# A SwiGLU kernel on one core: the steady order of its instructions searched anew, three sums moved from GpSimd to VectorE, and other work in the lead-in

## The chip, the core and the metric

The kernel runs on one core of one Trainium2 chip. The metric is the device time of one execution in microseconds (us), lower is better. The core has a matrix engine (TensorE, in the profile PE, with its weight loads shown apart as PEld), VectorE (DVE), ScalarE (ACT), GpSimd (POOL) and SyncE (SP), which here only issues DMAs. Each engine works through its own instructions in the order in which they were written, and waits at an instruction until what it needs is there.

## The reference, cut to what matters

```python
# x (8, 4096, 192): a causal convolution of 7 taps, the weights a softmax per head (8 heads of 24)
w = exp(weight - max); w = w / (w.sum(-1) + 1e-9)
y[b, s, h, g] = sum_k w[h, k] * x_pad[b, s + k, h, g]
# 32768 tokens of 192: RMS norm, then a gated feed-forward layer
xn = y / sqrt(mean(y * y) + 1e-6) * rms_g
g, val = xn @ w_gate, xn @ w_val          # 192 -> 1536 each
out = (g * sigmoid(g) * val) @ w_out      # 1536 -> 192
```

All inputs and the output are float32; the three weight matrices arrive as float64 words that the kernel converts itself.

## The kernel before

**Tiling.** The 32768 tokens are 32 pairs (0 to 31) of two 512-token tiles. The 1536 hidden units are 12 blocks of 128, taken as 6 double blocks, numbered j = 0 to 5. Pair 0 goes through plain matrix products: the gate loop `plain` (L1099) and the output loop `outer`. Pair 1 has plain gate products (L890, words a to d of the list PLAIN) and the output steps described below. Pairs 2 to 31 are the steady part: for each j the 2x2 block product (two token tiles by two hidden blocks) is done in the Strassen-Winograd manner.

**Gate products.** A *product* (`product`, L918; words P1..P7, Q1..Q4 and A, B, E with a cell letter) is 6 matmuls: three parts of a split operand, two halves of the rows (gate and value). The token operand is split into three parts by `split` (acts n, l, d: a cast on ACT at L683, a subtraction at L826, a multiply-subtract on DVE at L828) after the four sums x1..x4 of the token tiles (`x_sum`, L840). The weights come in pieces of 192 KB from a DRAM scratch `wd` through `ring`, ten slots in SBUF. `ring_load` (L798) fills a slot; SP issues it right behind the last product of the piece that held the slot, so each piece is asked for when the tenth-last one is done with. The first ten are issued at the word R (`ring_start`). The memory of the ring is lent before that: pair 2's tokens lie in it (`tokens`).

**Sums of the products.** Products of one j add up in PSUM in four cells a, b, c, d, each cell in one of four double banks (`open` takes one, `give` returns it). f1 (ACT, L683) copies cell a to b, f3 copies c to SBUF (two of the nine columns of `tt`, called s5), f4 (DVE, L989) makes c = b + s5, f5 makes d = b + s5. For each cell, g (ACT, L995) takes the silu of the gate half, m (DVE, L1002) multiplies it with the value half into `ht` and so frees the bank.

**Output.** The acts h1 to h4 (L972, DVE or POOL) sum cells of `ht` for the Strassen output; a *step* `o<form>.<k>` (`step`, `tiles`, `tile`, L945; form 1 to 7, k the double block) is 12 matmuls of 32 columns of weights. The forms accumulate in X, Y and Z; forms 1 and 7 with k = 0 start a bank afresh. C22 and C21 (DVE, L1019), the copies c1, s7, c2 (ACT) and the transposes T11 to T22 (DVE, L960) put the result together in `o_sb`; `st` (`leave`, L1051) stores it.

**The next pairs, meanwhile.** ld (`load_part`, L154) loads x of a pair two ahead, cv.0 to cv.6 (L453) are the taps for the next one, sq, red, pow, bc, mul the norm, pl (`put_away`, L1062) writes normed tokens to a DRAM scratch, ft (`fetch`, L654) reads them back as `xb`. ft.1 and ft.3 do nothing, since ft.0 and ft.2 fetch both halves.

**What sets the order.** From pair 1 on the order is written by hand. LINE is the order of a pair's work on PE. The lists FIRST (pass 1) and ORDER (each pass from 2 on) hold words that are carried out one after the other: `p3` emits the next three items of the pair's PE line; a word such as `Vf4.0` has the engine's letter (V DVE, G POOL, A ACT, S a DMA that SP issues), the act and its index; `+` and `++` mean the next pair or the one after it, `-` the one before; W is the next piece of the weights' preparation in the lead-in (`prepare`, which splits the weights and writes `wd`). A pass ends in the middle of its pair's output: pass w starts on PE with two products of pair w (P5.0, P1.0) and the six o3 steps of pair w-1, then come 66 products and 36 steps.

**Lead-in.** `first_loads` does not exist yet: `load_in` and `load_out` issue the first weight loads ahead of `conv_first`, which convolves pair 0 on ACT with PE's sums (taps 0, 2, 4) and on DVE (taps 1, 3, 5, 6, of which `give` = 2 heads are taken over from ACT's last). `hold` (L226) is a small copy that ties the first weight load to the x rows, since the load needs its result's place. START and LATER are two orders of the lead-in's parts; a letter O in LATER is one step of a converted w_out block (the result, `wo_sb`, is written at L337).

Of the kernel before, what the change touches and what calls it, by code (L numbers as in the profile page):

```python
# [20 lines left out]
def kernel(  # L21
# [10 lines left out]
    nc = tc.nc  # L32
# [3 lines left out]
    H, K = weight.shape  # L36
# [21 lines left out]
    PAIRS = B * NB  # L58
# [18 lines left out]
        "a5 b5 c5 d5",  # L77
    )
    ORDER = (
# [30 lines left out]
    )  # L110
    LINE = (
# [50 lines left out]
    def load_part(p, h, eng):  # L162

        if h == 0:
            x_sb[p] = xs.tile([P, TB + HALO, GS], F32, name="xh")
        load_head(p, p // NB, (p % NB) * PT, h, eng)
# [57 lines left out]
    def hold(t):  # L224

        nc.scalar.copy(out=t, in_=x0[:, -t.shape[1] :, 0])  # L226
# [163 lines left out]
    def conv_first(mine, share, give):  # L390
# [5 lines left out]
        for i, k in enumerate([theirs[0], mine[-1]] + theirs[1:]):  # L396
# [4 lines left out]
            if k == theirs[-1]:  # L401
                cuts = (0, H // 2, H - give)
# [11 lines left out]
        for k in mine:  # L414
            xk = t[:, k : k + NJ, :]
# [428 lines left out]
    class Pair:  # L844
        def __init__(self, p):
            self.p = p
            self.bk, self.o_sb, self.sg = {}, {}, {}
            self.open_half, self.turned = {}, [0, 0]
            self.line = self.products()
# [76 lines left out]
        def step(self, form, k):  # L926
# [3 lines left out]
            fresh = form in (1, 7) and k == 0  # L930
# [127 lines left out]
    def put_away(p, h, eng):  # L1058
        if h == 0:
            scr[p] = dram.tile([D, PT], F32, name="xd")  # L1060
# [101 lines left out]
    def done(it):  # L1162
# [14 lines left out]
        (30, "s"), (35, "v"), (45, "v"), (47, "O"), (50, "O"), (53, "O"), (55, "n"), (60, "t"),  # L1177
# [13 lines left out]
    load_in(0, nc.sync)  # L1191
    load_out(0)
    load_out(1)
    load_in(1, nc.sync)
# [111 lines left out]
```

## Time and profile before

| | |
|---|---|
| median of 3 runs | 2470.25 us (2469.66 to 2471.25) |
| profiled execution | 2473.39 us, its span 2471.6 |
| granted PE clock | 1.000 |
| PE matmuls | L918 12240 records, 1422.0 us busy; L945 16200 records, 1068.8 us |
| DVE | taps 336.6 us (186), silu products L1002 498.0 (744), f4/f5 295.8 (240) |
| POOL | sums L972 427.2 us (300), splits l.0 (L826) 69.7 (29), token norm L503 89.9 (30) |
| DMA | queue q1 425.21 MB, 66.5% of the 16 engines' span; 1440 ring loads, 240 put-aways, 192 loads of x |

How to read it: the span is from the first to the last instruction of the profiled execution, and that execution's time stands beside it. Busy shares are over the whole span. A matmul's record ends where a model puts it, so PE shows as busy through short waits; a weight load (PEld) shows the wait ahead of it. Each group in a view has its start, its busy time, the engine, what it writes and the line; in brackets is idle time ahead of it and what ended that. L683 and L972 are lines that several acts share, so they are told apart by their tiles.

### The profile page before, as it was taken

How to read it: one execution, taken by the hardware profiler on the slowest of the kernel's cores; microseconds unless marked ns; L12 is line 12 of the kernel's file. 1: busy time of each engine (PE TensorE's matmuls, PEld its weight loads, DVE VectorE, ACT ScalarE, POOL GpSimd, SP SyncE). 2: the span in 40 equal slices, each digit the busy share in tenths (PEclk: the TensorE clock that was granted, in tenths of full speed). 3: DMA queues.
4: the chain of work that ended last, by engine and by line, in shares of the span. 5: the costliest groups of instructions: out<-in, count | busy, mean ns of one | idle time of the engine just before them, and what ended most of it. 6: DMA issues, size and time to landing. Idle time of an engine off the chain costs nothing.

```text
span 2471.6 us, 69198 instructions
## 1 busy us (share of the span) xinstructions
PE 2452.5 (99%) x29136; PEld 1894.3 (77%) x29136; DVE 2024.1 (82%) x2530; ACT 1016.2 (41%) x1431; POOL 833.3 (34%) x624
## 2 busy tenths in 40 slices
PE   8999999999999999999999999999999999999999
PEld 5547778887777777877777778777787787777777
DVE  8688888889888789888888787888888888888864
ACT  6443434433344434344334344333444343443332
POOL 0541343423343323334333434233433333333322
PEclk9999999999999999999999999999999999999999
DMA  7364678666677666786667776666776666876653
GB/s 152 60 207 125 175 184 211 179 171 170 164 200 195 181 165 172 176 207 181 190 158 178 179 202 186 176 168 168 199 197 187 165 172 169 203 192 188 159 161 95
DMA packets 716392, 430.55 MB, mean 174 GB/s; under 512 B 510330, under 2 KB 702386, under 8 KB 716082
## 3 DMA queue, kind: packets, MB, share of 16 engines
q1 hardware_dynamic: 712336, 425.21, 66.5%
q8 instruction: 230, 3.77, 0.7%
q10 hardware_dynamic: 3746, 0.92, 0.2%
q14 instruction: 80, 0.66, 0.1%
HBM read 366.96 MB, written 58.98 MB: 172 GB/s over the span
## 4 chain that ended last, share of the span: by engine, by line
PE 90%; DVE 3%; DMA 3%; SPq 1%; issue 1%; POOL 1%; ACT 1%; DVEq 0%; POOLq 0%; ACTq 0%
PE ps L918 55%; PE ps L945 35%; DMA xb<-xd 1%; DMA ht<-in_moe_w_val_dram 1%; DMA ring<-wd 1%; SPq L154 0%; DVE ht L972 0%; POOL part L775 0%; SPq L238 0%; DVE ht L1117 0%; DVE ht L1002 0%; DVE part L771 0%; DVE y L453 0%; DMA x<-in_x_dram 0%; DVE ps L989 0%
## 5 line engine op out<-in xcount | busy, mean ns | idle before, releaser
L918 PE MATMUL ps<-part,ring 64*128 64x512 f32 x12240 | 1422.0, 389 | 2.6 <-DMA ring<-wd 1.9
L918 PEld LDWEIGHTS ps<-part,ring 64*128 64x128 f32 x12240 | 1152.9, 184 | 257.8 <-DVE ps L989 12.5
L995 ACT ACTIVATE tt<-ps 128x512 f32<-128x512 f32 x744 | 438.9, 599 | 715.8 <-PE ps L918 661.7
L1002 DVE TENSOR_TENSOR ht<-ps,tt 128x512 f32<-128x512 f32 x744 | 498.0, 686 | 254.3 <-ACT tt L995 252.2
L945 PE MATMUL ps<-ht,wo_sb 128*32 128x384 f32 (+2 forms) x7272 | 468.3, 380 | 0.8 <-POOL wo_sb L337 0.8
L972 POOL TENSOR_TENSOR ht<-ht 128x512 f32<-128x512 f32 x180 | 272.2, 1520 | 543.9 <-PE ps L945 536.4
L945 PE MATMUL ps<-ht,x 128*32 128x256 f32 (+2 forms) x6696 | 439.1, 379 | 1.3 <-DVE ht L972 1.3
L945 PEld LDWEIGHTS ps<-ht,wo_sb 128*32 128x32 f32 x7272 | 325.1, 110 | 114.5 <-issue 14.5
L945 PEld LDWEIGHTS ps<-ht,x 128*32 128x32 f32 x6696 | 299.6, 110 | 90.9 <-DVE ht L972 1.6
L989 DVE TENSOR_TENSOR ps<-ps,tt 128x1024 f32<-128x1024 f32 x240 | 295.8, 1233 | 54.3 <-ACT tt L683 22.8
L453 DVE SCALAR_TENSOR_TENSOR y<-xh,tp,y 128x1536 f32<-128x1536 f32 x186 | 336.6, 1810 | 0.2
L683 ACT COPY ps<-ps 128x1024 f32<-128x1024 f32 (+1 forms) x151 | 134.6, 891 | 408.0 <-PE ps L918 336.5
L972 POOL TENSOR_TENSOR hs<-ht 128x512 f32<-128x512 f32 x120 | 155.0, 1292 | 262.6 <-DVE ht L1002 262.6
L683 ACT COPY tt<-ps 128x384 f32<-128x384 f32 (+1 forms) x182 | 151.7, 833 | 218.6 <-PE ps L945 154.9
L482 POOL TENSOR_SCALAR r<-r 128x8 f32<-128x8 f32 x31 | 6.1, 197 | 504.5 <-DVE r L477 504.4
L945 PE MATMUL ps<-hs,x 128*32 128x128 f32 (+2 forms) x2232 | 161.4, 379 | 0.0
L972 DVE TENSOR_TENSOR ht<-ht 128x512 f32<-128x512 f32 x192 | 135.0, 717 | 15.2 <-PE ps L945 12.6
L945 PEld LDWEIGHTS ps<-hs,x 128*32 128x32 f32 x2232 | 106.9, 110 | 29.6
L828 DVE SCALAR_TENSOR_TENSOR part<-part,xb 128x1024 fp32r<-128x1024 f32 x87 | 120.1, 1381 | 0.0
L972 DVE TENSOR_TENSOR ht<-hs,ht 128x512 f32<-128x512 f32 x156 | 109.2, 747 | 11.3 <-PE ps L945 10.7
L826 POOL TENSOR_TENSOR part<-xb,part 128x1024 fp32r<-128x1024 f32 x29 | 69.7, 2403 | 124.0 <-PE ps L918 82.1
L503 POOL TENSOR_TENSOR xh<-y,s 128x1536 f32<-128x1536 f32 x30 | 89.9, 2995 | 15.1 <-DVE s L495 8.6
(133 smaller groups left out, 1417.6 us busy)
## 6 DMA issues: line engine op xcount, KB each, us to landing
ring<-wd SPq DMA_DIRECT2D x1440, 192.0 KB
xb<-xd SPq DMA_DIRECT2D x60, 512.0 KB
xd<-xh SPq DMA_DIRECT2D x240, 96.0 KB
xh<-in_x_dram SPq DMA_DIRECT2D x192, 105.0 KB
xb<-xd SPq DMA_DIRECT2D x60, 256.0 KB
out_dram<-o_sb SPq DMA_DIRECT2D x126, 96.0 KB
out_dram<-o_sb SPq DMA_DIRECT2D x62, 128.0 KB
wd<-part SPq DMA_DIRECT2D x5, 1152.0 KB
```

Source lines behind the costliest of these rows:

```text
L453: nc.vector.scalar_tensor_tensor(out=y, in0=xk, scalar=w, in1=y, op0=ALU.mult, op1=ALU.add)
L482: nc.gpsimd.tensor_scalar(out=r, in0=r, scalar1=s / D, scalar2=s * 1e-6, op0=ALU.mult, op1=ALU.add)
L503: e.tensor_tensor(out=yn[p].rearrange("p a t -> p t a"), in0=y, in1=ss[:].rearrange("p (t o) -> p t o", o=1).to_broadcast([P, TB, GS]), op ...
L683: nc.scalar.copy(out=dst, in_=src)
L826: e.tensor_tensor(out=split_of(g, 1).bitcast(F32R), in0=src, in1=high, op=ALU.subtract)
L828: nc.vector.scalar_tensor_tensor(out=split_of(g, 2).bitcast(F32R), in0=high, scalar=1.0 + SPLIT, in1=src, op0=ALU.mult, op1=ALU.subtract,)
L918: nc.tensor.matmul(out=self.both(j, c)[:, h, :], lhsT=left[HALF[h]], rhs=right[HALF[h]], start=(first and q == 0), stop=True, skip_group_c ...
L945: nc.tensor.matmul(out=self.acc(b)[i * Q : (i + 1) * Q, at : at + n], lhsT=left, rhs=cols, start=fresh, stop=True, skip_group_check=True, ...
L972: engine[eng].tensor_tensor(out=dst, in0=a, in1=b, op=op)
L989: nc.vector.tensor_tensor(out=self.both(j, c), in0=self.both(j, "b"), in1=s5, op=ALU.add)
L995: nc.scalar.activation(out=tt[:, t, :], in_=self.both(j, c)[:, 0, :], func=AF.Silu)
L1002: nc.vector.tensor_tensor(out=self.hv(j, "abcd".index(c)), in0=self.both(j, c)[:, 1, :], in1=tt[:, t, :], op=ALU.mult,)
```

## The change

ORDER and LINE are replaced by another order of the same work, and a list SECOND of its own is put in for pass 2. In the new LINE the steps o1.2 and o1.1 stand between the gate products Q2.5 and P4.5; before, all 36 steps followed all products. The steps may now come in any order within a form (`step` marks a bank as begun at its first use). x3, x4 and l.0 are on DVE instead of POOL in the steady passes, and all h4 sums on DVE; of the h sums DVE has 13 and POOL 11 as before, but others. All seven taps for pair w+1 now fall in pass w; before, the first three were done in pass w-1. Stores come one by one, An.0 (the cast of the tokens' first part) is moved behind Ac1, the empty ft.1 and ft.3 are dropped. In FIRST the taps of pair 3 and Vd.2+ (a split of pair 2) go out, Vma.1 and Vmb.1 stand ahead of some W; Vd.2 of pair 2 now comes in SECOND. PLAIN takes up the old order of the output steps, for pair 1. In the lead-in, `hold` copies on VectorE instead of ScalarE, the first weight loads are issued after DVE's first tap, one head (instead of two) of ACT's last tap goes to DVE, and three steps O come earlier.

The lists are cut here; of SECOND, which is nearly the same as ORDER, only the beginning stands.

```diff
     PLAIN = (
         "a0 b0 c0 d0 o1.0 a1 b1 c1 d1 o1.1 a2 b2 c2 d2 o1.2 a3 b3 c3 d3 o1.3 a4 b4 c4 d4 o1.4",
-        "a5 b5 c5 d5",
+        "a5 b5 c5 d5 o7.0 o7.4 o1.5 o7.3 o7.1 o7.2 o2.5 o2.0 o7.5 o6.1 o6.5 o6.0 o6.4 o6.2",
...
     ORDER = (
-        "p2 Vl.2 VC22- VT11- p3- Vd.4 VT22- VT21- Vcv3+ p3- Af1.0 Af3.0 VT12- p4 Aga.0 Vcv4+",
...
-        "Vma.4 Vf5.4 Agb.3 p3 Agd.4 Agc.4 Vmb.3 Vmd.4 Vmc.4 p2 Sft.2+ Sft.3+ Sst0.3- Sld.0++",
-        "Sft.4+ Sft.5+ Agb.4 Sld.1++ Sld.2++ Sst1.1- Gh1.2 Vmb.4 Gh1.1 Gh3.1 Gh1.0 p1 Sld.3++",
-        "Sst0.0- Gh3.2 Sld.4++ Sst0.1- Sld.5++ Af1.5 Sld.6++ Gh1.3 Sld.7++ p1 Af3.5 p2",
-        "Sst1.0- Sst1.2- Sst1.3- Vh1.4 Vh3.4 Vh3.0 Vf4.5 An.0+ Aga.3 p3 Vma.3 p2 Gl.0+ Gh3.3",
-        "Gx3+ Vf5.5 Aga.5 Agc.5 Vma.5 Vmc.5 p3 Vx1+ Agd.5 Agb.5 An.1+ Vx2+ p11 Vmd.5 Vh2.4",
-        "Vmb.5 Vd.0+ Vh1.5 Vh3.5 Vh2.3 Vh2.1 Vh2.5 Gx4+ Gh2.0 An.4+ Ac1 p5 Vh2.2 p1 An.3+ p4",
-        "An.2+ As7 p1 Ac2 Acv0++ Vh4.0 Vd.3+ Vd.2+ p11 Vh4.5 Vl.3+ Vh4.3 Vl.4+ Vcv1++ Vl.1+",
-        "Vcv2++ Vd.1+ p3 Gh4.1 VC21 Gh4.4 Gh4.2",
+        "VC22- p1 p1- VT21- p5- Acv0+ Af1.0 Vd.2 p1 VT22- Af3.0 Vl.2 p2 Vcv1+ VT12- Vf4.0",
...
+        "p1 Agb.4 Vmc.4 Vmb.4 p1 Agd.4 Spl.7+ p2 Af1.5 Sft.2+ Sft.0+ Vmd.4 p4 Af3.5 p1 Vf4.5",
+        "Gh1.3 Aga.5 Sst0.1- p1 Vh3.1 p2 Aga.3 Vma.5 p2 Gh1.4 Vma.3 Vf5.5 p4 Agd.5 Sld.6++ p2",
+        "Vmd.5 Agb.5 Gh3.4 p1 Vmb.5 p1 Vh1.5 Vx3+ Vh3.5 Gh3.3 Vh2.4 Agc.5 p1 Vx1+ Ac1 p1 Vx2+",
+        "p4 Sld.5++ Vx4+ Vh2.0 An.0+ p1 An.3+ Sst0.2- Gh2.1 Vh2.3 Sst1.3- An.4+ Gh2.2 Vd.0+",
...
+        "Vl.0+ Vh4.0 p1 Sft.5+ p2 Vl.4+ Vl.1+ p1 Vl.3+ VT11 Ac2 p2 Vh4.4 p2 VC21 p2 Vd.1+ p1",
+        "p1+ Vh4.5 An.2+",
+    )
+    SECOND = (
+        "p1 VC22- VT11- p3- VT22- Acv0+ VT21- Af1.0 Vd.2 p1- p1 p2- Af3.0 Vl.2 p1 VT12- p1",
...
     FIRST = (
...
-        "Vmc.0 W p1 Gpow+ W W W p1 W p1 Agd.0 W p1 Vmd.0 Vbc+ Vh1.0 p1 Gmul+ p1 Vh3.0 W",
-        "p1 Aga.1 W W W Vma.1 Vh2.0 p1 W W p1 Spl.0+ p1 Agb.1 Vmb.1 Spl.1+ p1 Spl.2+ W p1 Spl.3+ W",
+        "Vmc.0 W p1 Gpow+ W W W p1 W p1 Agd.0 W p1 Vmd.0 Vbc+ Vh1.0 p1 Gmul+ p1 Vh3.0 p1",
+        "Aga.1 Vma.1 p3 Agb.1 Vmb.1 W W W W Vh2.0 W W Spl.0+ Spl.1+ p1 Spl.2+ W p1 Spl.3+ W W",
...
-        "Vx2+ Vh1.4 p2 Gx4+ Vh3.4 Vh2.4 p1 Aga.5 Vma.5 An.3+ p1 An.2+ p1 Vd.3+ p1 Agb.5 Vd.2+",
-        "Vmb.5 Sld.0++ p1 Vl.3+ p2 Vl.1+ Agc.5 Vmc.5 Vd.1+ p1 Sld.1++ Vl.2+ p1 Sld.2++ Agd.5",
-        "p1 Vmd.5 p1 Vh1.5 p2 Ac1 Sld.3++ Vh3.5 Vh2.5 An.0+ An.4+ Gl.0+ Vd.0+ Vl.4+ p3 Sld.4++",
-        "Sld.5++ Sld.6++ Sld.7++ p1 Vh4.5 p1 Vh4.0 R Acv0++ p1 As7 p4 p2 Ac2 p1 Vcv1++ Vcv2++ Vh4.3",
-        "p9 Vh4.2 p2 Vh4.1 p2 VC21 p1 Vh4.4",
+        "Vh3.4 Vh2.4 p1 Aga.5 Vma.5 An.3+ p1 An.2+ p1 Vd.3+ p1 Agb.5 Vmb.5 Sld.0++ p1 Vl.3+",
+        "p2 Vl.1+ Agc.5 Vmc.5 Vd.1+ p1 Sld.1++ Vl.2+ p1 Sld.2++ Agd.5 p1 Vmd.5 p1 Vh1.5 p2",
+        "Ac1 Sld.3++ Vh3.5 Vh2.5 Sld.4++ Sld.5++ Sld.6++ Sld.7++ An.0+ An.4+ Gl.0+ Vd.0+",
+        "Vl.4+ p4 Vh4.5 p1 Vh4.0 R p1 As7 p6 Ac2 p1 Vh4.3 p9 Vh4.2 p2 Vh4.1 p2 VC21 p1 Vh4.4",
+        "Vd.4+ p1+",
     )
     LINE = (
-        "P5.0 P1.0 P2.0 Q1.0 P6.0 Ab.1 Bb.1 Eb.1 P7.0 Q2.0 Aa.1 P3.0 Ea.1 Ba.1 P4.0 Q3.0 Q4.0",
-        "P1.2 Ac.3 P5.2 Bc.3 Ec.3 P6.2 P2.2 Q1.2 Ad.3 Bd.3 P7.2 Q2.2 P3.2 Ed.3 Q3.2 Q4.2 P4.2",
-        "Ac.1 Bc.1 Ec.1 Ad.1 Bd.1 P1.4 Ed.1 P5.4 P6.4 Q1.4 Ab.3 P2.4 Bb.3 P7.4 Q2.4 P3.4 Eb.3",
-        "Q4.4 Q3.4 P4.4 P1.5 Aa.3 Ba.3 P5.5 P6.5 Ea.3 P2.5 Q1.5 P7.5 Q2.5 P3.5 Q3.5 Q4.5 P4.5",
-        "o1.0 o7.0 o1.4 o1.2 o1.3 o1.1 o7.4 o1.5 o7.3 o7.1 o7.2 o2.5 o2.0 o7.5 o6.1 o6.5 o6.0",
-        "o6.4 o6.2 o6.3 o2.3 o4.0 o4.3 o5.2 o5.3 o5.1 o4.5 o5.0 o4.4 o2.2 o4.1 o2.1 o5.4 o4.2",
-        "o5.5 o2.4 o3.3 o3.1 o3.0 o3.5 o3.2 o3.4",
+        "P5.0 P1.0 P6.0 Q1.0 P2.0 Ab.1 P7.0 P3.0 Q2.0 Bb.1 Eb.1 Q4.0 P4.0 Q3.0 Ac.3 Ec.3 Bc.3",
+        "Aa.1 P1.2 Ba.1 Ea.1 P5.2 P6.2 Q1.2 P2.2 Ac.1 Ec.1 Bc.1 P7.2 P3.2 Ad.3 Ed.3 Bd.3 Q2.2",
+        "Q3.2 Q4.2 P4.2 P1.4 Ad.1 Ed.1 Bd.1 P5.4 P6.4 Q1.4 P2.4 Ab.3 Eb.3 P7.4 Bb.3 Q2.4 P3.4",
+        "P4.4 Q3.4 Q4.4 P1.5 Aa.3 Ea.3 P5.5 P6.5 P2.5 Q1.5 Ba.3 P7.5 P3.5 Q2.5 o1.2 o1.1 P4.5",
+        "Q3.5 Q4.5 o1.5 o1.0 o1.3 o1.4 o7.1 o7.2 o2.2 o7.3 o2.0 o2.3 o7.0 o7.4 o2.1 o6.3 o7.5",
+        "o2.4 o6.2 o6.1 o4.1 o4.2 o4.4 o4.3 o6.5 o6.4 o6.0 o2.5 o4.5 o5.2 o5.1 o5.0 o4.0 o5.4",
+        "o5.5 o5.3 o3.0 o3.3 o3.1 o3.2 o3.5 o3.4",
     )
@@ load_part, put_away
-        if h == 0:
+        if p not in x_sb:
             x_sb[p] = xs.tile([P, TB + HALO, GS], F32, name="xh")
...
-        if h == 0:
+        if p not in scr:
             scr[p] = dram.tile([D, PT], F32, name="xd")
@@ hold
-        nc.scalar.copy(out=t, in_=x0[:, -t.shape[1] :, 0])
+        nc.vector.tensor_copy(out=t, in_=x0[:, -t.shape[1] :, 0])
@@ conv_first
-    def conv_first(mine, share, give):
+    def conv_first(mine, share, give, then):
...
-                cuts = (0, H // 2, H - give)
+                cuts = (0, H // 2, H - give) if give else (0, H // 2, H // 2 + 2, H)
...
         for k in mine:
+            if k == mine[1]:
+                then()
@@ class Pair, step
-            fresh = form in (1, 7) and k == 0
+            fresh = (b not in self.begun) and form in (1, 7)
+            self.begun.add(b)
@@ lead-in
-        (30, "s"), (35, "v"), (45, "v"), (47, "O"), (50, "O"), (53, "O"), (55, "n"), (60, "t"),
+        (30, "s"), (33, "O"), (35, "v"), (37, "O"), (44, "O"), (45, "v"), (55, "n"), (60, "t"),
...
-    load_in(0, nc.sync)
-    load_out(0)
-    load_out(1)
-    load_in(1, nc.sync)
-    conv_first((1, 3, 5, 6), 0, 2)
+
+    def first_loads():
+        load_in(0, nc.sync)
+        load_out(0)
+        load_out(1)
+        load_in(1, nc.sync)
+
+    conv_first((1, 3, 5, 6), 0, 1, first_loads)
@@ passes
     run([w for row in FIRST for w in row.split()], 1)
-    for w in range(2, PAIRS + 1):
+    run([w for row in SECOND for w in row.split()], 2)
+    for w in range(3, PAIRS + 1):
         run([w for row in ORDER for w in row.split()], w)
```

More of the change, by code (lines that the diff above doesn't have):

```diff
@@ L848, in __init__ @@
             self.open_half, self.turned = {}, [0, 0]
+            self.begun = set()
+            self.at = {}
             self.line = self.products()
```

39 rows, old and new, of tables (FIRST, ORDER, PLAIN, SECOND) are left out of this document.

## The prediction, on record before the changed kernel ran

> **What bounds the kernel now.** First the page's busy shares and its chain: TensorE (PE) is busy for all but 19 us of the span, and nine tenths of the chain that ended last are its own matmuls. Then the chain in order of time, for one late pass and the end of the lead-in. Then the weight loads in order of time, because a matmul's end is modelled and hides short waits, while a weight load that had to wait shows its idle time. Last, who held SP's queue and PE around the lead-in's end.
>
> ```profile
> PE 2452.5 (99%) x29136; PEld 1894.3 (77%) x29136; DVE 2024.1 (82%) x2530; ACT 1016.2 (41%) x1431; POOL 833.3 (34%) x624
> PE 90%; DVE 3%; DMA 3%; SPq 1%; issue 1%; POOL 1%; ACT 1%; DVEq 0%; POOLq 0%; ACTq 0%
> ```
> ```profile
> 196.01 2.89 DVE ht L972
> ...
> 198.95 15.16 PE ps L945 x184
> 214.10 1.60 PE ps L918 x12
> 215.71 4.04 PE ps L945 x48
> ...
> 2387.10 1.59 PE ps L918 x12
> 2388.68 4.04 PE ps L945 x48
> 2392.72 45.44 PE ps L918 x395
> 2438.16 23.54 PE ps L945 x288
> ```
> ```profile
> 1202.69 1.92 PEld L918 LDWEIGHTS ps<-part,ring 64*128 64x128 f32 x18 [0.28 <-DVE ps L989]
> 1205.01 16.85 PEld L918 LDWEIGHTS ps<-part,ring 64*128 64x128 f32 x150 [0.40 <-DVE ht L1002]
> 1222.01 15.52 PEld L918 LDWEIGHTS ps<-part,ring 64*128 64x128 f32 x138 [0.15 <-ACT ps L683]
> 1237.93 1.91 PEld L918 LDWEIGHTS ps<-part,ring 64*128 64x128 f32 x18 [0.39 <-DVE ps L989]
> ```
> ```profile
> SPq L798 <- DVE part L828: 14.7, 1, 14.7
> ...
> PE ps L918 <- DMA ring<-wd: 1.9, 5, 0.8
> PE ps L945 <- DVE ht L972: 1.3, 1, 1.3
> ```
>
> A pass is four stretches on PE: 2 gate products, 6 output steps, 66 gate products, 36 output steps (12, 72, 396 and 432 matmuls; a few records are missing). Undisturbed, the 150 loads from 1205.01 to 1222.01 are 75 matmul pairs in 17.0 us: 0.227 a pair, 0.68 a product. The two output stretches differ by 30 steps and 19.5 us: 0.65 a step. So the 66 products need 44.95 us, and the thirty long blocks of this trace take 45.44 to 46.83, 45.76 on average. What exceeds is 0.81 a pass, 24.4 us in all. Of it 0.2 a pass is the block's own entry and exit (seen also in the short block, which nothing delays: 1.59 for 6 pairs, 1.36 bare). About 0.03 is jitter. **The remaining 0.58 a pass, 17.4 us in all, is waits, and this is the most that any order can win here.** The loads name them: f4/f5 (L989), a silu product (L1002) that frees a PSUM bank, an ACT copy. The dearest in the bad passes starts as An.0, which holds ACT for the xb fetch in mid-block; f5.5 then comes late.
>
> **Part by part, steady passes.** (1) Switches. The new LINE puts o1.2 and o1.1 between Q2.5 and P4.5, so PE changes from products to steps and back once more in each pass: 31 more switches there and back, counted over both programs (60 product blocks of this kind become 91). One costs 0.22 (short block, 1.59 less 1.36) plus 0.14 (4.04 less 6 times 0.65): 0.36. Together **+11.1 us**. Nothing hides it; PE is the bound.
>
> (2) Waits that go. In the old order Q3.5 follows P7.5 by two products (1.4 us), while f5.5 (1.23) must come between, behind DVE's m.3. The new one has P3.5, Q2.5, o1.2 and o1.1 between P7.5 and P4.5: P7.5's result is there 0.2 us after its end, then DVE has Vh3.1 behind it, m.5 and m.3 (0.60 each), f5.5 (1.23): done 2.0 us after P7.5, and P4.5 starts 3.0 after it. An.0 moves behind Ac1 into the output steps, so the fetch (6.16 us from issue in the chain) has over 6 us before its first reader Vx3, and it is issued behind the gate block's last ring load instead of ahead of five. I laid DVE's other gate work in its new order, each item by its row, (f 1.14 from start to start, m 0.60, tap 1.73, split 1.14, h 0.60), against PE's: f4.0 ends 0.6 before P7.0 needs it, f5.0 0.5 before Q4.0, banks for P1.2, P5.2, P1.4, P5.4, P1.5 and P5.5 come free 0.5 to 1.7 early. The tightest is f3.5 then f4.5 before P7.5, 0.3, the distance it has now without a wait. From m.5 to C22 DVE has 21.1 us of work for 21.9 until o3.0 writes X: 0.7 left. All margins being positive but small, I take 15.5 of the 17.4: **-15.5 us**; ends -8 (half of the waits come back) and -17.4.
>
> (3) The sums that move. DVE gets x3, x4 and l.0 (0.69, 0.69, 1.22), POOL loses them (1.28, 1.30, 2.40). Meetings go: DVE's h ran 1.12 beside POOL's against 0.68, its split 1.71 against 1.22. DVE's load stays near 61 of 74.7 us. Cover: the idle fifth of DVE; without it the 2.6 us would show, as far as it exceeds the 0.7 left before o3.0. **0.**
>
> (4) SP's queue. Loads of the ring (48 a pass) are issued when the tenth-last piece is done with. In the old order each has 6.1 us or more before its use; in the new one six have 4.1 (pieces used from P2.2 through Ac.1, Ec.1 and Bc.1 to P7.2) and four 4.8 to 5.5. Stores go from clusters to single places, and one (0.4 to 1.4 us of issue) stands behind these six. A load alone lands 2.35 us after issue (those at 1284 and 1285, by their semaphores), one queued behind others within half a us 4.2. The six come 0.68 apart: margin 1.5. **0**, bounds 0 to +7.5 (first rival). Put_away moves 8 us later with Gmul, its issues (0.55 each, eight) now beside loads of 5.5 lead; about 0.7 remains.
>
> **The boundary of pass 1 and 2.** Pair 2's tokens lie in the memory that becomes the ring. FIRST no longer has Vd.2+; SECOND has Vd.2, which reads those tokens, so the first ring load waits for it; before, it waited for a split that ended at 200.9. P5.0 of pair 2 stands on PE before the last o3 steps and needs slot 0. From the end E of the steps (214.1 before), DVE has by its rows Vh4.4 from E+0.1 (0.61), Vd.4 (1.14), C22 (0.47), T11, T22, T21 (0.56 each) and Vd.2 (1.22): done at E+5.2. The same first load at 200.9 landed after 2.8, the second, for P1.0, 4.7 after the first issue. So P1.0 starts at E+10.0 instead of E+0.7: **+9.2 us**, ends +7.6 (both land as a lone load) and +9.6. Queued behind it are SP's other loads, which PE gates anyway, and on PE everything.
>
> By the fit in the Trainium skill's SBUF — State Buffer, "The DMA setup-cost knee" (2 us plus bytes at 436 GB/s), a load of 196608 bytes takes an estimated 2.45; the stall would be 7.7 and the sum 1.5 lower. The rows at 200.9 speak against it for loads in a burst, those at 1284 for it.
>
> **Lead-in.** (5) hold on DVE: ACT's taps now start with the first x rows, 7.5 instead of 9.1, ACT takes one tap more; DVE has one tap less (0.33) and the copy more (about 0.1), and no wait of 0.11 for PE's sums: -0.35. SP's weight loads start when DVE reaches the copy, some 0.4 later; they are read 6 us after landing, so 0; ends -0.5, +0.4. (6) wo_sb's conversion three places earlier: the 0.8 of PE waiting for L337: -0.8, at worst 0. (7) Vma.1 and Vmb.1 ahead of four W: of the 1.4 that L890 waits for L1002, -1.0; ends 0, -1.4. (8) PE's 1.3 on L972: h3.5 ran 2.88 beside POOL's l.0 (2.37). Without Vd.2 ahead, h3.5 is over 0.3 before l.0 starts: -1.25; ends 0, -1.3. Dropped taps for pair 3 only spare DVE. Together **-3.4 us**, ends 0 and -4.
>
> **Sum**: +11.1 - 15.5 + 9.2 - 3.4 = +1.4. Tail: T12 after the last o3 ends both, 0. The profiled execution has a span of 2471.6 and 2473.39 in all; the median of the runs is 2470.25, 1.35 under that span. So 2470.25 + 1.4 = **2471.6 us**.
>
> **Rivals.** *Slower by late ring loads.* Place: P2.2 to P7.2, loads with 4.1 us. If one a pass lands after more than about 3.9, PE waits some 0.15 and restarts at 0.11 (a block's entry): 0.25 times 30, 7.5 us: 2479. For: loads took 4.2 in bursts; a store precedes. Against: these come singly.
>
> *Faster, the boundary costs nothing*: if the first ring load did not wait for Vd.2, or DVE were far ahead: 2471.6 - 9.2 = 2462.4. Against: Vh4.4 waits for the last o2 step, so DVE cannot be ahead.
>
> *The change does not do what it says*: f5.5 still comes late (some row of DVE between P7.5 and P4.5 is a us longer), the switches are paid for nothing: 7.5 of the 15.5 lost, 2479 again.
>
> *Meetings were the limit*: their removal lets PE run without waits and the switch costs half: 2471.6 - 1.9 - 5.5 = 2464. Only the loads' idle times could show it, and they name L989 and L1002, not L972.
>
> **Numbers.** Forecast 0.54 (2466 to 2476 by its own bounds); late loads 0.18; late f5.5 0.1; boundary free 0.1; meetings 0.03; something dearer, 0.05. A measurement of this kernel tells 0.2%, 4.9 us, from no change. Of the forecast's own spread nearly all lies within that. Faster 0.16 (both fast rivals and 0.03 of the forecast), same 0.5, slower 0.34 (the slow ones and the forecast's upper edge). Range 2463 to 2481: forecast, both slower rivals and the fastest one's edge.
>
> **What would show it.** Right: in a pass's chain five or six PE pieces more, a block of 6 pairs x 3 (18 matmuls) of 2.27, an o stretch of 12 of 1.4, the 62- or 63-product block within 0.3 of its bare 42.2 or 42.9; loads without L989 in their idle times; one wait of PE of 9 us, of L918 for the ring, near 211, with SP held by the split's line. Wrong: ring waits in most passes; no boundary wait; or long blocks with 0.5 of waits left.

## The result, and the profile after

The changed kernel takes 2501.62 us (median of 4 runs, 2500.22 to 2506.63) against 2470.75 us before. The ratio is 1.0131, with a 95% interval of 1.0119 to 1.0144: slower by 1.3%, 31 us. The forecast of 2471.6 us and its range up to 2481 were both missed. The profiled execution is the longest of the four: 2506.63 us, its span 2504.8, which is 33.2 more than the profiled span before.

In the changed kernel the lines have moved by some twenty: L942 is the gate product (L918 before), L970 the output step, L820 the ring's load, L1087 the put_away, L676 the fetch, L850 DVE's split, L1014 f4 and f5, L1027 DVE's silu product, L997 the h sums, L705 ACT's copies. In the kernels of the experiments they differ from these by one to three; the two experiments that start from the kernel before have its lines plus two.

First the page's busy line and its chain, after:

```profile
PE 2466.5 (98%) x29136; PEld 1937.1 (77%) x29136; DVE 2027.5 (81%) x2617; ACT 1033.8 (41%) x1431; POOL 631.6 (25%) x537
...
PE 91%; DMA 6%; DVE 2%; SPq 1%; issue 0%; ACT 0%; POOL 0%; DVEq 0%
```

DMA has gone from 3% to 6% of the chain. The waits, after (who waited for whom: us in all, times, longest), say which DMA, and what SP stood at:

```profile
PEld ps L942 <- DMA ring<-wd: 26.6, 39, 1.4
...
PE ps L942 <- DMA ring<-wd: 20.7, 29, 7.7
...
PEld ps L942 <- DVE ps L1014: 5.4, 10, 1.8
```
```profile
SPq L676 <- DMA xd<-xh: 39.5, 29, 2.5
...
SPq L820 <- DVE part L850: 31.9, 1, 31.9
```

Before, PE waited 1.9 us for the ring, in 5 places, and f4/f5 were the first name among the loads' waits (12.5 us). Now the ring is the first, and f4/f5 come to 5.4. The wait of 7.7 us is the one at the boundary of pass 1 and 2; the chain in order of time shows what led to it, VectorE's split Vd.2 and then the first ring load:

```profile
214.79 1.12 DVE part L850
215.91 0.02 SPq L820
215.93 0.03 issue
215.96 2.43 DMA ring<-wd
218.39 0.14 issue
218.53 2.93 PE ps L942 x12
```

Now the chain in order of time for one pass, and the loads of PE at the same place:

```profile
1213.71 39.04 PE ps L942 x337
1252.75 3.63 DMA ring<-wd
1256.39 0.04 issue
1256.43 0.96 PE ps L942 x6
1257.39 1.44 PE ps L970 x16
1258.83 2.29 PE ps L942 x18
```
```profile
1242.96 12.89 PEld L942 LDWEIGHTS ps<-part,ring 64*128 64x128 f32 x114
1256.43 0.53 PEld L942 LDWEIGHTS ps<-part,ring 64*128 64x128 f32 x6 [0.59 <-DMA ring<-wd]
```

The stretches look as forecast (18 matmuls in 2.27 to 2.29, the inserted steps 1.44). What was not forecast is the load issued at 1252.75, which landed 3.63 later, for Q2.5, the last product ahead of o1.2. What SP did ahead of it:

```profile
1242.09 1.42 SPq L820 DMA_DIRECT2D ring<-wd  x1
1243.61 1.24 SPq L1087 DMA_DIRECT2D xd<-xh  x2
1244.93 0.56 SPq L820 DMA_DIRECT2D ring<-wd  x1
1245.55 0.53 SPq L1087 DMA_DIRECT2D xd<-xh  x1
1246.18 0.56 SPq L820 DMA_DIRECT2D ring<-wd  x1
1246.79 0.53 SPq L1087 DMA_DIRECT2D xd<-xh  x1
1247.37 0.60 SPq L1076 DMA_DIRECT2D out_dram<-o_sb  x1
1248.01 1.20 SPq L1087 DMA_DIRECT2D xd<-xh  x2
1249.31 1.04 SPq L820 DMA_DIRECT2D ring<-wd  x2
1250.40 0.54 SPq L1087 DMA_DIRECT2D xd<-xh  x1
1251.03 1.04 SPq L820 DMA_DIRECT2D ring<-wd  x2
1252.12 0.54 SPq L1087 DMA_DIRECT2D xd<-xh  x1
1252.75 1.04 SPq L820 DMA_DIRECT2D ring<-wd  x2
```

In 11.7 us SP issues 9 ring loads, 8 put_aways and a store, one after the other; from 1243.61 on they follow each other at 0.44 to 0.72, without a pause. Towards the end of the block PE frees a slot every 0.68, so each put_away puts the loads behind it back by most of its own issue. I set every ring load of the trace against the end of the product that freed its slot and the start of the product that reads it (medians of 29 pairs, us; the last column from the starts of PE's matmuls):

| load for | kernel | lead | issued after slot is free | landing | passes of 30 in which PE waited |
|---|---|---|---|---|---|
| P2.5 | before | 6.64 | 0.09 | 3.89 | 0 |
| P2.5 | after | 5.28 | 1.96 | 2.65 | 7 |
| Q2.5 | before | 5.96 | 0.04 | 4.77 | 0 |
| Q2.5 | after | 6.74, the wait in it | 2.70 | 3.66 | 19 |
| P7.2 | after | 3.91 | 0.04 | 3.42 | 1 |

The landings at the end of the block are shorter than before. The issue is what is late.

Late issue alone is not new. By the same reckoning the old order has it too, behind its own put_aways: the loads for P4.4 and P1.5 were issued 2.93 and 2.96 after their slots were free, but with a lead of 7.3, and PE did not wait for them. In the new order the lateness meets leads of 5.3 to 6. The trace of after holds a control as well: its last pass has no tokens left to put away, and there, with the same order of products, the loads for P2.5, P7.5 and Q2.5 are issued 0.04, 0.04 and 0.61 late, land in 4.22, 3.88 and 2.93, and PE waits for none.

The whole difference of the two profiled executions, from the starts of PE's matmuls: up to the end of the steps ahead of pair 2 the change is 3.2 faster; from there to the start of pair 2's long block it needs 17.1 instead of 5.6 (+11.5); from there to the end 24.9 more. The thirty long blocks of products exceed their bare time and one entry by 31.9 us, before by 17.7 (+14.2), and 11.4 are the switches (2.28 for three products that take 2.04 undisturbed, 1.44 for two steps that take 1.29, thirty times); the long block of pair 2 is a product shorter (0.7), because that product now stands ahead of it. So the sum closes at 33.2. Of the 31.9, 22.5 stand ahead of P2.5, P7.5 and Q2.5 with what follows them, 4.5 around P7.2.

### The profile page after: what moved, and what is told of

It is laid out like the page before. It is cut to its first block, busy times and chain, and to the rows that moved or that the text cites. A ratio compares the mean times of both kernels' runs of the same rounds, so it can differ in the third digit from the quotient of the medians.

```text
span 2504.8 us, 68920 instructions
## 1 busy us (share of the span) xinstructions
PE 2466.5 (98%) x29136; PEld 1937.1 (77%) x29136; DVE 2027.5 (81%) x2617; ACT 1033.8 (41%) x1431; POOL 631.6 (25%) x537
## 4 chain that ended last, share of the span: by engine, by line
PE 91%; DMA 6%; DVE 2%; SPq 1%; issue 0%; ACT 0%; POOL 0%; DVEq 0%
PE ps L942 52%; PE ps L970 35%; DMA ring<-wd 5%; PE ps L1124 2%; PE ps L914 1%; DMA ht<-in_moe_w_val_dram 0%; SPq L174 0%; DMA x<-in_x_dram 0%; DVE ht L997 0%; DVE ps L1014 0%; DVE o_sb L985 0%; DVE ht L1027 0%; DVE part L793 0%; DMA ht<-in_moe_w_gate_dram 0%; SPq L258 0%
## 5 line engine op out<-in xcount | busy, mean ns | idle before, releaser
L942 PE MATMUL ps<-part,ring 64*128 64x512 f32 x12240 | 1433.0, 390 | 24.1 <-DMA ring<-wd 20.7
L942 PEld LDWEIGHTS ps<-part,ring 64*128 64x128 f32 x12240 | 1197.7, 184 | 238.2 <-DMA ring<-wd 26.6
L1027 DVE TENSOR_TENSOR ht<-ps,tt 128x512 f32<-128x512 f32 x744 | 496.7, 686 | 257.4 <-ACT tt L1020 249.8
L970 PE MATMUL ps<-ht,wo_sb 128*32 128x384 f32 (+2 forms) x7272 | 454.9, 382 | 0.7 <-DVE tt L1044 0.7
L970 PE MATMUL ps<-ht,x 128*32 128x256 f32 (+2 forms) x6696 | 419.2, 379 | 0.0
L970 PEld LDWEIGHTS ps<-ht,wo_sb 128*32 128x32 f32 x7272 | 316.6, 110 | 123.6 <-issue 32.8
L1014 DVE TENSOR_TENSOR ps<-ps,tt 128x1024 f32<-128x1024 f32 x240 | 295.8, 1233 | 129.0 <-ACT tt L705 93.9
L970 PEld LDWEIGHTS ps<-ht,x 128*32 128x32 f32 x6696 | 289.0, 110 | 92.6 <-issue 0.8
L705 ACT COPY tt<-ps 128x384 f32<-128x384 f32 (+1 forms) x182 | 151.9, 835 | 267.6 <-PE ps L970 223.5
L997 POOL TENSOR_TENSOR hs<-ht 128x512 f32<-128x512 f32 x150 | 194.5, 1297 | 101.5 <-DVE ht L1027 101.3
L705 ACT COPY ps<-ps 128x1024 f32<-128x1024 f32 (+1 forms) x151 | 134.2, 889 | 128.0 <-PE ps L942 57.8
L997 DVE TENSOR_TENSOR ht<-ht 128x512 f32<-128x512 f32 x252 | 172.8, 697 | 10.7 <-PE ps L970 10.5
L997 POOL TENSOR_TENSOR ht<-ht 128x512 f32<-128x512 f32 x120 | 155.3, 1294 | 90.3 <-DVE ht L1027 88.0
L970 PE MATMUL ps<-hs,x 128*32 128x128 f32 (+2 forms) x2232 | 141.8, 379 | 0.0
L705 ACT CAST part<-xb 128x1024 fp32r<-128x1024 f32 x87 | 91.1, 1048 | 98.4 <-DMA xb<-xd 98.4
L970 PEld LDWEIGHTS ps<-hs,x 128*32 128x32 f32 x2232 | 101.5, 110 | 30.3
L850 DVE SCALAR_TENSOR_TENSOR part<-part,xb 128x1024 fp32r<-128x1024 f32 x87 | 105.1, 1208 | 1.3 <-ACT part L705 1.3
L848 DVE TENSOR_TENSOR part<-xb,part 128x1024 fp32r<-128x1024 f32 x87 | 105.4, 1212 | 0.0
```

Source lines behind the costliest of these rows:

```text
L705: nc.scalar.copy(out=dst, in_=src)
L848: e.tensor_tensor(out=split_of(g, 1).bitcast(F32R), in0=src, in1=high, op=ALU.subtract)
L850: nc.vector.scalar_tensor_tensor(out=split_of(g, 2).bitcast(F32R), in0=high, scalar=1.0 + SPLIT, in1=src, op0=ALU.mult, op1=ALU.subtract,)
L942: nc.tensor.matmul(out=self.both(j, c)[:, h, :], lhsT=left[HALF[h]], rhs=right[HALF[h]], start=(first and q == 0), stop=True, skip_group_c ...
L970: nc.tensor.matmul(out=self.acc(b)[i * Q : (i + 1) * Q, at : at + n], lhsT=left, rhs=cols, start=fresh, stop=True, skip_group_check=True, ...
L997: engine[eng].tensor_tensor(out=dst, in0=a, in1=b, op=op)
```

## The experiments

**Four put_aways behind the urgent loads.** In ORDER, and the same in SECOND:

```diff
- Sst0.4- Agb.3 Spl.0+ Vf5.4 Spl.1+ Gh3.2 Vmb.3 p1 Agc.4 p1 Spl.2+ p1 Agb.4 Vmc.4 Vmb.4 p1 Agd.4 Spl.7+ p2 Af1.5 Sft.2+ Sft.0+
+ Sst0.4- Agb.3 Vf5.4 Gh3.2 Vmb.3 p1 Agc.4 p1 p1 Agb.4 Vmc.4 Vmb.4 p1 Agd.4 p2 Af1.5 Spl.0+ Spl.1+ Spl.2+ Spl.7+ Sft.2+ Sft.0+
```

> The changed kernel with four of the eight put_aways of each pass (pl.0, pl.1, pl.2, pl.7) moved behind the last weight load that is due in the pass, just ahead of the two fetches; nothing else. In the profile of the changed kernel, waits of PE for the ring in the long product block are 31 us in 30 passes, 26 of them ahead of P2.5, P7.5 and Q2.5, whose loads SP issues 2.0 to 2.7 us (medians) after their slot is free. Theory Q (SP's queue: eight put_aways and a store at about 0.55 each stand among these loads): the loads are issued within 1 us, the 26 us go, about 2477 (2472 to 2483), the few waits near P7.2 stay. Theory M (memory traffic: the packets of put_away and fetch make landings long, 3.0 to 3.7 instead of 2.4): the traffic moves by only 3 to 8 us and now lies beside the fetch, so less than half goes, 2489 to 2500. Theory P (the leads of the new product order are too short by themselves): nothing goes, 2500.

Measured: 2483.28 us, ratio 1.0058 (1.0043 to 1.0073) to the kernel before; 18.3 less than the changed kernel. The excess of the long blocks falls from 31.9 to 9.9. SP's queue of this kernel around the end of a pass's block, and the chain there:

```profile
1240.35 1.68 SPq L819 DMA_DIRECT2D ring<-wd  x3
1242.08 2.59 SPq L1086 DMA_DIRECT2D xd<-xh  x4
1246.72 1.38 SPq L675 DMA_DIRECT2D xb<-xd  x2
1248.20 1.80 SPq L819 DMA_DIRECT2D ring<-wd  x4
```
```profile
1210.68 37.15 PE ps L941 x324
1247.82 1.44 PE ps L969 x16
1249.26 2.26 PE ps L941 x18
```

The four put_aways stand together behind the last urgent loads, no DMA is left in this pass's chain. Over the passes the load for Q2.5 is issued 0.04 after its slot is free (2.70), that for P2.5 0.41 (1.96), while they land no faster than in the changed kernel (3.68 and 3.01): PE waits for none of the three in any pass. This is theory Q, at a time just past the upper end of what it gave (2483); theories M and P, which held landings or leads to blame, gave 2489 and more.

**The same four issued by ACT.**

```diff
- Spl.0+ ... Spl.1+ ... Spl.2+ ... Spl.7+
+ Apl.0+ ... Apl.1+ ... Apl.2+ ... Apl.7+
```

> The changed kernel with the same four put_aways at their present places, but issued by ACT instead of SP. The transfers stay where they are, only SP's time goes. Theory Q: loads for P2.5, P7.5 and Q2.5 are issued within 1 us of their slot, the 26 us of waits go as in the run with the put_aways moved, 2475 to 2483, unless ACT's own time (four issues) delays a silu. Theory M: landings stay long, waits stay, 2494 to 2502. Theory P: 2500.

Measured: 2492.22 us, ratio 1.0089 (1.0074 to 1.0104): 9.4 less than the changed kernel, above what Q gave and just under M's. Q2.5's load is issued 1.42 late instead of 2.70, and its wait is nearly gone (2 passes of 30), but P2.5's is still issued 2.10 late, and two new waits show. The waits of SP, then of PE's loads, in this kernel:

```profile
SPq L675 <- DMA xd<-xh: 56.1, 29, 4.1
SPq L819 <- DMA xd<-xh: 41.3, 34, 2.4
```
```profile
PEld ps L941 <- ACT ps L704: 11.8, 18, 1.7
```

SP's loads now stood 41.3 us for the put_aways' transfers, and ACT, held by its four issues, was late with f1.5 (L704) for P6.5, 9.5 us in all. The trace shows what ties SP to ACT's transfers: the kernel's DMAs take eight completion semaphores in turn, whichever engine issues them, and an issue waits until the DMA that used its semaphore before has landed. Some 24 of the 41.3 us are such waits, and in the rest too SP waits on a semaphore that one of ACT's put_aways holds. For instance SP stood 1.7 us, up to 263.23, ahead of a ring load, until the put_away that ACT had issued at 259.89 with the same semaphore was done. The run took SP's time away and put two other waits in its place; it does not tell Q from M by itself, the run before it does.

**The split of pair 2 back in FIRST.**

```diff
- "... Agb.5 Vmb.5 Sld.0++ p1 Vl.3+",
+ "... Agb.5 Vd.2+ Vmb.5 Sld.0++ p1 Vl.3+",
```

> The changed kernel with Vd.2+ back in FIRST, ahead of the ring's start, as it stood before (SECOND then skips it). Theory of the boundary: the first ring load no longer waits for pair 2's split. In the two traces the long product block of pair 2 begins 8.3 us later after the change, although the steps ahead of it end 3.2 us earlier: 11.5 us, of which 0.4 is the extra switch. They go, and 1.3 of h3.5 beside l.0 may come back: 2490 to 2493. Rival (the loads would have been late anyway, held by something else on SP or by traffic): 2498 to 2502. The steady passes are the same in both.

Measured: 2497.54 us, ratio 1.0114 (1.0099 to 1.0129), 4.1 less than the changed kernel. That is above the 2490 to 2493 of the theory and just under its rival's 2498. The profile speaks for the theory: pair 2's long block begins at 219.44 instead of 228.01, 8.6 earlier, and of PE's 7.7 us of waiting for the ring nothing is left there, only 0.8 for the sum C22. The median shows half of it. The excess of the long blocks is 30.0, little less than in the changed kernel. So the stall was at this boundary and came from the split. What it is worth at the end lies between 4 and 9, and the runs do not settle it: executions of one of these kernels differ by 6 to 8 us among themselves, and the intervals of the two ratios overlap.

**Both repairs.** The two diffs together.

> The changed kernel with both repairs: four put_aways behind the last urgent weight load, and Vd.2+ back in FIRST. If the two costs are separate, their effects add: 2483.3 of the first repair, less the 8.6 us by which pair 2's long block began earlier in the second one's trace, 2474.7 (2472 to 2478). If they share a cause, less: 2480. Left over the kernel before would then be the switches (11.4 by the rows: 30 blocks of 18 matmuls at 2.27 instead of 2.04, 30 stretches of 24 at 1.44 instead of 1.29) and some 10 of waits in place of 17.7, less 3 of the lead-in.

Measured: 2479.76 us (2473.98 to 2481.17, 8 runs), ratio 1.0033 (1.0023 to 1.0044). Against the first repair alone the second brings 3.5, again about half of what the block's start shows (219.57 against 226.84); the put_aways bring 17.8 on top of the other repair, 18.3 without it. So the cost of the put_aways is measured twice and firm. The total is above the 2472 to 2478 that was given for two separate costs and at the 2480 given for a shared cause; but a shared cause would have made the put_aways' gain smaller here, and it is the same. What fell short is the gain from the split.

This run also shows what is left of the change without its two costs: from the start of pair 2's long block to the end it needs 6.7 us more than the kernel before. The switches cost 11.4 and new waits in the o3 steps 2.1; the waits in the long blocks fall by only 6.1, to 11.7, and pair 2's long block is a product (0.7) shorter.

**Without the insertion.** On the kernel with both repairs, and so in SECOND:

```diff
- LINE: Q2.5 o1.2 o1.1 P4.5 Q3.5 Q4.5 o1.5
+ LINE: Q2.5 P4.5 Q3.5 Q4.5 o1.2 o1.1 o1.5
- ORDER: Vma.5 p2 Gh1.4 Vma.3 Vf5.5 p4 Agd.5 Sld.6++ p2 Vmd.5
+ ORDER: Vma.5 p1 Gh1.4 Vma.3 Vf5.5 p3 Agd.5 Sld.6++ p4 Vmd.5
```

> As the run with both repairs, but o1.2 and o1.1 stand behind Q4.5 with the other steps, so that PE does not change to steps and back within the product block; all words else in place. Theory F (the insertion is paid for by f5.5): in the repaired run f5.5 ends 2.04 us after P7.5 and P4.5 starts 2.74 after it; without the two steps P4.5 could start at 1.36 and waits to 2.1, plus 0.1 of restart: 0.83 lost, 0.38 of switches gained, 0.45 a pass, 13 us slower than the repaired one, about 2488. Theory S (the switch is a pure loss, f5.5 would be moved ahead by itself): 11.4 faster, 2463.

Measured: 2492.55 us, ratio 1.0094 (1.0079 to 1.0109): 12.8 more than with the insertion, where theory F gave 13. The waits of PE in this kernel (L1012 is f4/f5):

```profile
PEld ps L940 <- DVE ps L1012: 30.6, 33, 1.8
...
PE ps L940 <- DVE ps L1012: 16.9, 31, 1.3
```

f5.5 ends 1.83 us after P7.5 (medians of the trace) and P4.5 starts at 1.89, where it could at 1.2 (not at 1.36, as I had it; the next run has one product more between them and starts at 1.88 without a wait): 0.71 there and 0.11 behind the next pair of matmuls are lost in 29 passes, 24 us. In this order of VectorE's work the insertion is worth more than its switches cost.

**Another product in the steps' place.** Instead of o1.2 and o1.1 the product Ea.3 fills the time:

```diff
- LINE: P1.5 Aa.3 Ea.3 P5.5 P6.5 P2.5 Q1.5 Ba.3 P7.5 P3.5 Q2.5 o1.2 o1.1 P4.5 Q3.5 Q4.5 o1.5
+ LINE: P1.5 Aa.3 P5.5 P6.5 P2.5 Q1.5 Ba.3 P7.5 P3.5 Q2.5 Ea.3 P4.5 Q3.5 Q4.5 o1.2 o1.1 o1.5
- ORDER: Vmd.4 p4 Af3.5 ... Vh3.1 p2 Aga.3 Vma.5 p2 Gh1.4 Vma.3 Vf5.5 p4 Agd.5 Sld.6++ p2 Vmd.5
+ ORDER: Vmd.4 p3 Af3.5 ... Vh3.1 p2 Vma.5 p1 Gh1.4 Vf5.5 p1 Aga.3 Vma.3 p3 Agd.5 Sld.6++ p4 Vmd.5
```

> As the run without the insertion, but the product Ea.3 (which nothing waits for soon) is moved from behind Aa.3 to between Q2.5 and P4.5, with silu and product of cell a of j = 3 behind f5.5. Three products (2.04 us) then lie between P7.5 and P4.5, and DVE has one item of 0.60 less ahead of f5.5, which should end 1.4 to 1.7 after P7.5. Theory F: neither a wait nor a switch, 11.4 us less than the run with both repairs: about 2463 (2461 to 2467), faster than the kernel before. Rival (a later silu of this cell delays a bank or o1.3 instead, or f4.5 comes late for P7.5, which now follows 0.68 earlier): 2468 to 2476.

Measured: 2483.5 us, ratio 1.0053 (1.0036 to 1.007), slower than the run with both repairs: the rival's way, and past its range of 2468 to 2476. f5.5 ends 1.42 after P7.5 and P4.5 does not wait for it; but P5.5, which now comes a product earlier, waits for a bank that a silu product frees, 0.25 and 0.11 in 29 passes, 10.7 us:

```profile
PEld ps L940 <- DVE ht L1025: 14.7, 30, 0.7
```

**m.3 behind f5.5.** Without the insertion:

```diff
- ORDER: Gh1.4 Vma.3 Vf5.5 p3
+ ORDER: Gh1.4 Vf5.5 Vma.3 p3
```

> As the run without the insertion (both repairs, o1.2 and o1.1 with the other steps), with one word moved: DVE's product m.3 of cell a goes behind f5.5 instead of ahead of it. There f5.5 started 0.61 after P7.5 and ended at 1.83, and PE waited 0.71 and 0.11 in each of 29 passes, 24 us. Theory F (DVE's place for f5.5 decides): f5.5 starts at 0.04 and ends at 1.28, as in the kernel before, P4.5 can start at 1.36, nearly all of the 24 us go: 2468 to 2471 (2492.5 less 24). Rival (m.3 late now delays a bank or o1.3): 2475 to 2485.

Measured: 2484.02 us, ratio 1.0053 (1.0039 to 1.0067): 8.5 less than with m.3 ahead, not 24. The time lies in the rival's range (2475 to 2485), but not for its reason, a bank freed late by m.3. f5.5 starts 0.20 after P7.5 rather than at 0.04 and ends at 1.43, and P4.5, at 1.49 in place of 1.2, still loses 0.31 and 0.11, 12 us in all. Without a third piece of work in between, f5.5 (1.23) doesn't fit behind P7.5.

**With the tap and two stores moved as well.**

```diff
- Aga.0 p2 Vcv6+ Vma.0 p2 Vf5.0 Agc.0 p2 Vmc.0 ... Vcv3+ Sst1.1- p1 ... Af3.2 Sst0.0- Vf4.2
+ Aga.0 p2 Vma.0 p2 Vf5.0 Agc.0 Vcv6+ Sst1.1- Sst0.0- p2 Vmc.0 ... Vcv3+ p1 ... Af3.2 Vf4.2
```

> As the run with m.3 behind f5.5, and further: tap cv.6 behind f5.0 instead of ahead of f4.0's neighbour m.0 (in the runs without the insertion PE waits 0.08 and 0.08 for f5.0 ahead of Q4.0 in nearly every pass, 4.7 us), and the stores st.1.1 and st.0.0 brought forward, away from the six loads with 3.9 of lead (2 to 3 us of ring waits in a profile). Theory: another 5 to 7 us, 2461 to 2466, faster than the kernel before by 4 to 9. Rival (tap later means m.c.0 late, or the stores now meet other loads): as the run before it, 2468 to 2471, or slower.

Measured: 2487.68 us (2481.81 to 2489.0), ratio 1.0065 (1.0053 to 1.0078): no gain, where 2461 to 2466 were expected. The waits ahead of Q4.0 go (4.9 us), the ring's near P7.2 fall from 3.2 to 1.9, and the rival's wait comes: P5.2 waits 0.20 and 0.11 for a bank in 28 passes, 9.0 us.

**The sums back on GpSimd.** On the kernel with both repairs, in ORDER and SECOND:

```diff
- Vx3+ ... Vx4+ ... Vl.0+
+ Gx3+ ... Gx4+ ... Gl.0+
```

> As the run with both repairs (2479.8), but x3, x4 and l.0 are back on GpSimd at the same places of the order, which frees 2.6 us of VectorE in a pass and brings back meetings of the two engines' sums. My step 3 (the move is worth nothing either way, the idle fifth of VectorE covers it): 2477 to 2483. Rival (meetings of VectorE and GpSimd cost PE time): slower, 2484 to 2492, with VectorE's h sums and split longer than 0.7 and 1.22 and PE waiting for L997's sums or for the splits.

Measured: 2589.19 us, ratio 1.048 (1.0464 to 1.0496), 109 more than with the sums on VectorE, about 100 past both the theory and its rival. Lines of the groups (idle time and what ended it at the end), then waits, of this kernel:

```profile
L968 PE MATMUL ps<-ht,x 128*32 128x384 f32 (+2 forms) x6696 | 415.5, 381 | 91.0 <-DVE ht L995 53.0 <-POOL ht L995 37.1
```
```profile
POOL tt L860 <- DMA xb<-xd: 239.6, 29, 10.1
```

All of it lies in the output steps: the stretch of 34 steps goes from 22.24 us to 25.99 on average, 3.75 in each of 29 passes. Two things come together. GpSimd stands at x3 for the fetch, 8.3 us a pass, with its h sums queued behind it, and PE waits for these. And VectorE's sums and splits run longer: 1015 ns instead of 702 for the most frequent h sums, 1727 instead of 1218 for the splits of the token sums. Over the whole execution its h sums (L995) take 422 us instead of 293 and its splits (L848) 244 instead of 183, and the longer ones are those that run beside an instruction of GpSimd (on average 1.18 against 0.63, and 2.29 against 0.89). That is what the rival named, at a multiple of its price. VectorE's h sums show no wait for GpSimd of their own. How the 109 us divide between the queue and the meetings this run does not show.

**The lead-in alone, on the kernel before.** `hold`, `first_loads`, give 1 and the three O steps; all lists as before.

> The kernel before with the lead-in changes alone: hold on VectorE, weight loads issued after DVE's first tap, give 1 instead of 2, three O steps earlier; all word lists as before. By the two traces the output steps of pair 0 begin 0.56 us earlier and lose 0.9 of waiting for wo_sb: about 1.5 us less, 2468.8; at most 0.3 of it would be lost again if the first block of pair 1 waits for a bank. Rival (the gain is taken back where pair 1's stretch waits for VectorE anyway): 2470.3.

Measured: 2467.23 us, ratio 0.9992 (0.9983 to 1.0002): the size is as expected and not told from no change. Pair 0's steps begin 0.34 earlier and take 31.40 instead of 32.36, and pair 2's long block starts 1.28 earlier.

**An.0 late in the old order.** On that kernel:

```diff
- Vf4.5 An.0+ Aga.3 p3 Vma.3 p2 Gl.0+ Gh3.3 ... Vmb.5 Vd.0+ Vh1.5 ... Gh2.0 An.4+ Ac1 p5 Vh2.2
+ Vf4.5 Aga.3 p3 Vma.3 p2 Gh3.3 ... Vmb.5 Vh1.5 ... Gh2.0 Ac1 An.0+ An.4+ Gl.0+ p5 Vd.0+ Vh2.2
```

> The kernel before with the lead-in changes, and with An.0, Gl.0 and Vd.0 of ORDER moved behind Ac1 into the output steps (An.0 as the change has it), so that ACT does not stand still for the fetch in mid-block. Theory: the irregular waits of the long block that begin at An.0 go, some 4 to 6 of the 17.7 us of the trace of before: 2462 to 2464 (2467.2 was the lead-in alone). Rival: those waits have another cause, 2467.

Measured: 2509.83 us, ratio 1.016 (1.0145 to 1.0175), 43 slower than without it: the theory fell. The long blocks' excess stayed (14.6 against 12.5), and in the short product blocks and in the steps new waits came that name the sums C22 and C21 (L1021), here on PE's loads of the products:

```profile
L920 PEld LDWEIGHTS ps<-part,ring 64*128 64x128 f32 x12240 | 1153.2, 184 | 267.9 <-DVE tt L1021 19.0
```

None of these kernels is clearly faster than the one before.

## Why the prediction was wrong, by its steps

**The step that failed is (4), SP's queue.** It priced the ring's lateness at 0, with 7.5 as the upper bound; the trace of after has 27 us of it (22.5 and 4.5), and moving four put_aways takes 18 of the 31 us back. Three things in it were off. The place: the rival looked at the six loads with the shortest lead (P2.2 to P7.2; 3.9 in the trace of after, for the 4.1 it gave), and these cost 4.5 us, in some six passes; the loads that cost five times as much have the longer leads of 5.3 to 6. The reckoning: it did name the eight put_aways "beside loads of 5.5 lead" and each issue's 0.55, and left a margin of 0.7, by setting one issue against one lead. But the issues add up: eight put_aways, a store and the loads themselves need SP for longer than PE takes to free the slots, so the lateness grows from load to load, to 1.96 at P2.5 and 2.70 at Q2.5. The row to read was SP's queue over the whole stretch, what it must issue against how long PE takes, not the lead of each load. And the lead itself: 5.3 less 3 of landing leaves 2.3, and that much was used up. The forecast also said that the fetch was issued behind the block's last ring load; it is, and it did no harm, though SP stands 1.4 us a pass for the last put_away's landing there (39.5 in 29).

**The boundary: right in kind and place.** The first ring load waits for Vd.2 (31.9 us of SP, one time), Vd.2 ends 5.0 after the steps (forecast 5.2). PE then stood 7.7, not 9.2: P5.0 began when the first load had landed, 2.43 after its issue, and P1.0 found its own there in time. The Trainium skill's SBUF — State Buffer, "The DMA setup-cost knee", put a load at an estimated 2.45 and the stall at 7.7; for the first load the trace agrees with it. What the step did not have is the clock. PE's granted clock over the stall, columns as in the table of windows (the third figure from the end is the clock):

```profile
211.00:213.00 2.00, 0.00 (x0) 0.00 (x0) 2.00 (x3) 0.00 (x0) 0.00 (x0) 1.00 0.00 0
213.00:215.00 2.00, 0.00 (x0) 0.00 (x0) 2.00 (x8) 0.00 (x0) 0.00 (x0) 0.83 0.00 0
215.00:217.00 2.00, 0.00 (x0) 0.00 (x0) 0.90 (x1) 0.00 (x0) 0.00 (x0) 0.50 0.02 2
...
223.00:224.00 1.00, 1.00 (x16) 0.79 (x12) 0.00 (x0) 0.47 (x1) 0.00 (x0) 0.50 1.05 389
224.00:225.00 1.00, 1.00 (x20) 0.74 (x16) 0.00 (x0) 0.00 (x0) 0.00 (x0) 0.71 0.55 196
225.00:226.00 1.00, 1.00 (x18) 0.56 (x12) 0.00 (x0) 0.00 (x0) 0.00 (x0) 1.00 0.05 8
```

The first 12 matmuls after the stall take 2.86 instead of 1.58, the next 48 matmuls, of steps, 4.28 instead of the 2.74 of the run with both repairs: 2.8 us more. Stall and clock make 10.5, a little over the step's upper end of 9.6. The median gave back only 4.1 and 3.5 where the stall was removed, and what became of the rest stays open.

**(1), the switches: right.** 11.1 forecast, 11.4 found, with the pieces at 2.27 to 2.29 and 1.44 (2.27 and 1.4 forecast).

**(2), the waits that go: right for f5.5, too large as a sum.** f5.5 ends 2.01 us after P7.5 in the trace of after (2.0 forecast) and P4.5 starts at 3.15, ring waits in it, or at 2.74 without them (3.0 forecast); taking the insertion out costs 12.8. Of the 17.7, some 5 came back at other places in the trace of after, so about 13 went in place of 15.5. But with the ring's waits out of the way more come back: 9.9 are left in the run with the put_aways moved and 11.7 in the one with both repairs, ahead of P7.0, Q4.0 and others. So only 6 to 8 went, under the step's lower end of 8, and less than the switches cost. With the put_aways moved and the stall gone the kernel is still 9.5 slower than before. That the ring's waits had hidden these others, by giving VectorE time, is argued and not tested.

**(3), the sums that move: right in this direction,** PE waits nowhere for x3, x4 or l.0 on VectorE. That the reverse move costs 109 in the new order was not seen: the step set the meetings of the two engines at nothing, and it did not look at what stands behind x3 in GpSimd's queue.

**The lead-in: right in sum, wrong inside.** -3.4 forecast, -3.2 found: convolution -0.6 (-0.35), wo_sb -0.9 (-0.8), h3.5 -1.4 (-1.25). Vma.1's move gained 1.4 at once, but the next block of pair 1 waited 1.15 longer, -0.25 in place of -1.0. Alone it can't be told from no change.

The first rival, late ring loads, was the right one; its price, 7.5 against 27, was wrong by more than three times. Its own sentence against it, that the loads come singly, held for the place at which it looked.

## What to carry to other kernels

A queue that issues transfers is an engine with a throughput of its own: over each stretch, add up all that it has to issue (here 18 issues of about 0.6 in 11.7 us) and set the sum against the time in which the consumer frees its slots; a lead that is long enough for each load alone does not help once the queue runs behind by more than the lead has to spare. Work that has time (here put_aways) goes behind the last load that has none. And an order with all margins under a microsecond answers each repair with the next wait: the three runs here that took one wait away (Ea.3 moved, m.3 moved, the tap moved) each had 9 to 12 us of another, at a bank or in the same place.

## What the runs showed of the hardware that was not expected

A stall of PE costs more than its length. In the trace of after the granted clock went from 1.00 to 0.50 some 3.5 us after PE's last matmul, and it came back 6.0 us after PE had started again (worked out from the windows above). In the run with the put_aways moved, whose stall was as long, the two figures are 4.1 and 3.4, with the put_aways on ACT 3.6 and 2.9. The windows of the run with the put_aways moved:

```profile
219.00:222.00 3.00, 3.00 (x18) 1.84 (x19) 0.00 (x0) 0.30 (x1) 0.00 (x0) 0.50 0.99 286
222.00:226.00 4.00, 4.00 (x66) 2.85 (x62) 0.00 (x0) 1.63 (x2) 0.00 (x0) 0.99 0.71 252
```

The Trainium skill's TensorE: Matmul & The Clock Gate, Part 1, "What's actually happening", states half rate after an idle window of about 3.4 us and full rate after about 3.4 us of sustained work, on a window that runs freely. The time at half rate was 10.2, 6.8 and 6.8 us in the three runs, three times and twice 3.4, which fits whole windows of that length. The three drops and the returns after 3.4 and 2.9 agree with the page roughly, the return after 6.0 does not.

Each wait in a product block is paid a second time behind the next pair of matmuls, with 0.11 (3.2 us in 29 passes in each of three runs).

ACT's issues of put_aways were not free for SP: with four of them on ACT, SP's ring loads stood 41.3 us for their transfers, which they did not do before. By the trace this comes from the completion semaphores that the two engines' DMAs share, so it belongs to this program.
